# Linear attention feeding an expert layer: reciprocals spread over the features by DMA through DRAM, attention steps moved to the end of each block, transposes one a slot, row copies on ScalarE

## The chip, the cores and the metric

The kernel runs on one core of one Trainium2 chip. The metric is the device time of one execution in microseconds (us), lower is better. Each number is a median of several executions, compared with executions of the kernel before on the same chip. A ratio is the mean time of one kernel's fast runs over the mean of the other's fast runs of the same rounds, so it is not quite the ratio of the medians quoted beside it. A change counts as faster or slower only beyond 2%; below that the verdict is "same".

## The reference, cut to what matters

```
# attention: q, k, v are (batch 8, heads 8, seq 576, dim 64)
q_p = [relu(q) * cos, relu(q) * sin]       # 128 features; k_p likewise
kv  = sum over s of k_p x v ;  z = sum over s of k_p
x   = (q_p @ kv) / (q_p @ z + 1e-6)        # one denominator per batch, head and position
# x as 4608 tokens x 512 features (8 heads x 64), then 8 experts, F = 1024:
P   = sinkhorn(exp(x @ w_gate))            # 8 iterations
out = sum over e of P[:, e] * (relu(x @ w1[e]) @ w2[e])
```

The change is about the division. A denominator belongs to a head and a position, while the product to be divided has 64 features of that head. Its reciprocal therefore has to be repeated over 64 partitions before VectorE can multiply.

## The kernel before

The first part of the kernel runs in seven blocks. Block j does the first expert's two products for 512 tokens: slots 0 to 7 are eight groups of four matmuls (w1) with a ReLU on ScalarE into `hT`; slots 8 to 15 are eight groups of four matmuls (w2) whose results go to `acc`. Between the slots the pieces of the attention of batch b = j + 1 are put in: `prep_*` (cos and sin products on VectorE), `turn` (transposes of q, three matmuls each), `sums` (kv and z), `denominators`, and four `attend`s, one for each pair of heads. Work on TensorE, VectorE and ScalarE is bound to the written order. The loads that GpSimd issues are not.

```python
def denominators(b):
    ...                                    # 24 matmuls into den_ps
    ve.tensor_scalar(out=den, in0=den_ps, scalar1=1e-6 / XS, ...)
    ve.reciprocal(out=den, in_=den)        # 96 x 192: row 32*j + r is head r % 8, third j
    ve.tensor_copy(out=hi, in_=den)        # fp16 high part
    ve.scalar_tensor_tensor(out=hl, ...)   # high part or remainder, by row
    hls[b] = hl

def attend(b, hk):
    parts = ((0, 2 * C3), (2 * C3, C))     # 384 and 192 positions
    rb_ps = [ps_s.tile(...) for _ in parts]          # ps_s: four PSUM banks
    rb = rb_pool.tile([P, C * HP], FP32)
    for i, (c0, c1) in enumerate(parts):
        for j in range(c0 // C3, c1 // C3):
            te.matmul(out=rb_ps[i][...], lhsT=spread[0:96, j, hk], rhs=hls[b])   # spread by matmul
        se.copy(out=rb[:, c0 * HP : c1 * HP], in_=rb_ps[i][...])
    num_ps = [ps_s.tile(...) for _ in parts]
    for i, (c0, c1) in enumerate(parts):
        ...                                          # two matmuls: kv x q, one for each head
        ve.tensor_tensor(out=xT[...], in0=num_ps[i][...], in1=rb[...], op=ALU.mult)

# schedule of block j, b = j + 1 (cut)
at(j, 0, prep_q, b, 3); at(j, 1, prep_kv, b, 3)
at(j, 1, sums, b, 0);   at(j, 3, sums, b, 1)
for i, (hk, k_) in enumerate(turns[2:]):
    at(j, i // 2, turn, b, hk, k_)                   # two transposes a slot
at(j, 5, denominators, b)
for hk in range(HK):
    at(j, FT + 2 * hk, attend, b, hk)                # slots 8, 10, 12, 14
...                                                  # loads at slots 0, 2; prep of b + 1 at slots 6 to 15
# end of a w2 group: even rows by ScalarE, odd rows by VectorE
se.copy(out=acc(g), in_=y_ps) if g % 2 == 0 else ve.tensor_copy(out=acc(g), in_=y_ps)
```

The softmax here doesn't subtract the row's maximum and nothing guards it: scores larger than these inputs give would overflow.

Of the kernel before, what the change touches and what calls it, by code (L numbers as in the profile page):

```python
# [10 lines left out]
FP32 = mybir.dt.float32  # L11
F16 = mybir.dt.float16
# [13 lines left out]
def kernel(  # L26
# [10 lines left out]
    nc = tc.nc  # L37
    P = nc.NUM_PARTITIONS

    B, H, S, D = q.shape  # L40
    E, Dm, F = moe_w1.shape
    N = B * S
    HP = P // 2
    assert Dm == H * D and 2 * D == P and H % 2 == 0 and S % HP == 0
    HK = H // 2
    C = S // HP
# [3 lines left out]
    FT = F // P  # L50
    TCH = 512
# [12 lines left out]
    dram = ctx.enter_context(tc.tile_pool(name="dram", bufs=2, space=bass.MemoryType.DRAM))  # L64
# [6 lines left out]
    G_LO = NG - 4  # L71
    acc_lo = acc_pool.tile([P, G_LO, Dm], FP32, name="acc_lo")
    acc_hi = acc_pool.tile([P, NG - G_LO, Dm], FP32, name="acc_hi")

    def acc(g):
        return acc_lo[:, g, :] if g < G_LO else acc_hi[:, g - G_LO, :]
# [69 lines left out]
    def ffn2(hT, w, c0, g, y_ps, fts):  # L146

        for ft in fts:
            te.matmul(
                out=y_ps,  # L150
                lhsT=hT[:, ft, c0 : c0 + P],
                rhs=w[1][:, ft, :],
                start=(ft == 0),
                stop=(ft == FT - 1),
            )
        if FT - 1 in fts:

            if g % 2 == 0:
                se.copy(out=acc(g), in_=y_ps)
            else:  # L160
                ve.tensor_copy(out=acc(g), in_=y_ps)
# [10 lines left out]
    with ExitStack() as p1:  # L172
        hA = p1.enter_context(tc.tile_pool(name="hA", bufs=1))
        cs_pool = p1.enter_context(tc.tile_pool(name="cs_pool", bufs=1))
# [2 lines left out]
        qp_pool = p1.enter_context(tc.tile_pool(name="qp_pool", bufs=3))  # L177
        qT_pool = p1.enter_context(tc.tile_pool(name="qT_pool", bufs=6))
        kv_pool = p1.enter_context(tc.tile_pool(name="kv_pool", bufs=2))
        rb_pool = p1.enter_context(tc.tile_pool(name="rb_pool", bufs=2))  # L180
        ps_y = p1.enter_context(tc.tile_pool(name="ps_y", bufs=2, space=bass.MemoryType.PSUM))
        ps_s = p1.enter_context(tc.tile_pool(name="ps_s", bufs=4, space=bass.MemoryType.PSUM))

# [4 lines left out]
        def load(b, half, names="qkv"):  # L188
# [25 lines left out]
            out=ident[:], in_=ones_sq[:], pattern=[[-1, P]], compare_op=ALU.is_equal,  # L214
# [13 lines left out]
        def keep_busy(n):  # L228
# [12 lines left out]
            out=wrap[:], in0=gidx[:], scalar1=float(S), scalar2=None, op0=ALU.is_ge  # L241
# [3 lines left out]
            out=sval[:], in0=wrap[:], scalar=-float(S), in1=gidx[:],  # L245
# [13 lines left out]
        C3 = C // 3  # L259
# [7 lines left out]
        with nc.allow_low_precision("sums of zeros and ones"):  # L267
            ve.tensor_reduce(
                out=lo[:], in_=rows[:, :, 1, :], axis=AX.XY, op=ALU.add, negate=True
# [3 lines left out]
                out=sel[:], in0=rows[:, 0:3, 0, :], in1=rows[:, 0:3, 1, :], op=ALU.add  # L273
            )
        ve.tensor_copy(
            out=spread.rearrange("p j hk hh d -> p (j hk hh) d"),
            in_=sel[:].rearrange("p j h -> p (j h)").unsqueeze(2).to_broadcast([P, 3 * H, D]),
# [9 lines left out]
        ve.tensor_copy(out=wg[:], in_=wg_ld[:])  # L287


        kps, qps, qTs, kvs, hls = {}, {}, {}, {}, {}  # L290
        v_augs = [cs_pool.tile([P, C, D + 2], F16, name=f"v_aug{i}") for i in range(4)]
        for t in v_augs:
            ve.memset(t[:, :, D : D + 1], 1.0 / XS)

# [82 lines left out]
        def denominators(b):  # L377

            zsel = kvs[b][1]
            den_ps = ps_s.tile([P, 512], FP32, name="small_ps")  # L380
            for h in range(H):
                hk, hh = h // 2, h % 2
                for j in range(3):
                    te.matmul(
                        out=den_ps[32 * j : 32 * j + 32, 0 : C3 * HP],
                        lhsT=zsel[:, h, :],
                        rhs=qTs[b, hk][:, j * C3 : (j + 1) * C3, hh * HP : (hh + 1) * HP],
                        start=(h == 0),
                        stop=(h == H - 1),
                    )  # L390
            den = kv_pool.tile([96, C3 * HP], FP32, name="den")
            ve.tensor_scalar(
                out=den[:], in0=den_ps[0:96, 0 : C3 * HP], scalar1=1e-6 / XS, scalar2=None,
                op0=ALU.add,
            )
            ve.reciprocal(out=den[:], in_=den[:])

            hi = kv_pool.tile([96, C3 * HP], F16, name="hi")
            ve.tensor_copy(out=hi[:], in_=den[:])
            hl = kv_pool.tile([96, C3 * HP], F16, name="hl")  # L400
            ve.scalar_tensor_tensor(
                out=hl[:], in0=hi[:], scalar=lo[0:96], in1=den[:], op0=ALU.mult, op1=ALU.add
            )
            hls[b] = hl

        def attend(b, hk):

            parts = ((0, 2 * C3), (2 * C3, C))
            rb_ps = [ps_s.tile([P, 512], FP32, name="small_ps") for _ in parts]
            rb = rb_pool.tile([P, C * HP], FP32, name="rb")  # L410
            for i, (c0, c1) in enumerate(parts):
                for j in range(c0 // C3, c1 // C3):
                    te.matmul(
                        out=rb_ps[i][:, (j * C3 - c0) * HP : ((j + 1) * C3 - c0) * HP],
                        lhsT=spread[0:96, j, hk].rearrange("p hh d -> p (hh d)"),
                        rhs=hls[b][:],
                        start=True,
                        stop=True,
                    )
                se.copy(out=rb[:, c0 * HP : c1 * HP], in_=rb_ps[i][:, 0 : (c1 - c0) * HP])  # L420
            num_ps = [ps_s.tile([P, 512], FP32, name="small_ps") for _ in parts]
            for i, (c0, c1) in enumerate(parts):
                for hh in range(2):
                    te.matmul(
                        out=num_ps[i][hh * HP : (hh + 1) * HP, 0 : (c1 - c0) * HP],
                        lhsT=kvs[b][0][:, hk, hh, :],
                        rhs=qTs[b, hk][:, c0:c1, hh * HP : (hh + 1) * HP],
                        start=True,
                        stop=True,
                    )  # L430
                ve.tensor_tensor(
                    out=xT[:, hk, b * S + c0 * HP : b * S + c1 * HP],
                    in0=num_ps[i][:, 0 : (c1 - c0) * HP],
                    in1=rb[:, c0 * HP : c1 * HP],
                    op=ALU.mult,
                )
# [22 lines left out]
        NS = 2 * FT  # L459
        todo = {}  # L460

        def at(block, slot, fn, *args):
            todo.setdefault((block, slot), []).append((fn, args))

        turns = [(hk, i) for hk in range(HK) for i in range(3)]
# [17 lines left out]
        for hk in range(HK):  # L483
# [5 lines left out]
            if hk < 2:  # L489
                prep_q(0, hk + 2)  # L490
        denominators(0)
        keep_busy(36)

# [6 lines left out]
        for hk in range(HK):  # L500
# [7 lines left out]
            for kt in ((), (0,), (1,), (2, 3))[hk]:  # L508
                for ft, h_ps in enumerate(first_ps):
                    te.matmul(  # L510
                        out=h_ps[:],
# [10 lines left out]
        ahead = (  # L522
            (prep_k, 0), (prep_q, 0), (prep_k, 1), (prep_kv, 0), (prep_q, 1), (prep_k, 2),
            (prep_kv, 1), (prep_q, 2), (prep_k, 3), (prep_kv, 2),
        )
        for j in range(B):
            b = j + 1
            if j == 0:

                at(0, 4, lambda: begun.append(sums_begun(1, 0)))  # L530
                at(0, 5, lambda: sums_made(1, 0, begun[2]))
                at(0, 6, lambda: begun.append(sums_begun(1, 1)))
                at(0, 7, prep_q, 1, 0)
                at(0, 7, prep_q, 1, 1)
                for hk in range(HK):
                    for i in range(3):
                        at(0, 7 + hk, turn, 1, hk, i)
                    if hk == 0:
                        at(0, 7, lambda: sums_made(1, 1, begun[3]))
                    if hk < 2:  # L540
                        at(0, 7 + hk, prep_q, 1, hk + 2)
                at(0, 10, denominators, 1)
                at(0, 11, gates, 0)
                for hk in range(HK):
                    at(0, min(13 + hk, 15), attend, 1, hk)
            elif b < B:
                at(j, 0, prep_q, b, 3)
                at(j, 1, prep_kv, b, 3)
                at(j, 1, sums, b, 0)
                at(j, 3, sums, b, 1)  # L550
                for i, (hk, k_) in enumerate(turns[2:]):
                    at(j, i // 2, turn, b, hk, k_)
                at(j, 5, denominators, b)
                for hk in range(HK):
                    at(j, FT + 2 * hk, attend, b, hk)
            if j:
                at(j, 6, gates, j)
            if b + 1 < B:
                for half in range(2):
                    at(j, 2 * half if j else 3, load, b + 1, half)  # L560
                for i, (fn, hk) in enumerate(ahead):
                    at(j, NS - 10 + i if j else 11 + i // 2, fn, b + 1, hk)
                for hk, k_ in turns[:2]:
                    at(j, NS - 1, turn, b + 1, hk, k_)
        y_pss = {}
        for j in range(B - 1):
            if j:
# [494 lines left out]
    while stream:  # L1062
        _, pair, name = stream.pop(0)
# [32 lines left out]
```

## Time and profile before

| what | before |
|---|---|
| time | 1003.37 us (1002.86 to 1003.73, 4 runs) |
| span of the profiled run, granted TensorE clock (1 is full speed) | 1000.8 us, 0.997 |
| blocks 0 to 6 | 23.66, 22.25, 22.19, 22.29, 22.20, 22.29, 21.85 us |
| from the first `H` of the next part to the end | 815.5 us |

A block is measured in the timeline, from ScalarE's first ReLU into `hT` to that of the next block. The seven blocks lie between 28.5 and 185.3 us. The change touches only blocks 1 to 6 and what is prepared for them.

The page of the kernel before, its first table: busy time and share of the span of each engine.

```profile
PE 981.3 (98%) x8062; PEld 689.3 (69%) x8062; DVE 829.2 (83%) x1862; ACT 574.7 (57%) x1284; POOL 60.3 (6%) x82
```

The chain of waits of the kernel before (start, length, what). TensorE's (PE) groups carry the chain. At the end of each block it passes through VectorE (DVE) for a while; the block's period can be read from the repeats of the same piece.

```profile
72.22 0.98 PE y_ps L100 x4
...
73.84 0.75 DVE k_p L100
...
93.80 0.61 PE small_ps L100 x7
94.42 0.98 PE y_ps L100 x4
95.42 0.37 DVE acc_lo L100
96.03 0.75 DVE k_p L100
...
118.33 0.75 DVE k_p L100
```

The period is 22.2 to 22.3 us. In the timeline of TensorE, one attend looks as follows: three spreading matmuls with `hl`, the four with `kv_sb`, then the next w2 groups.

```profile
113.48 0.41 PE L100 MATMUL small_ps<-hl,acc_hi 96*128 96x192 f16 x3
113.83 0.44 PE L100 MATMUL small_ps<-q_pT,kv_sb 128*64 128x384 f16 x4
114.19 1.90 PE L100 MATMUL y_ps<-w2e,hT 128*128 128x512 f16 x8
```

The three spreading matmuls put off what follows by 113.83 - 113.48 = 0.35 us. They are what the change takes away from TensorE, four times a block. The SP queue has no DMA to issue in this part.

### The profile page before, as it was taken

To read this page: it belongs to the slowest core of one execution; us is meant where nothing else is said; L and a number is where in the kernel's file an instruction comes from. 1 tells how busy PE (TensorE), PEld (TensorE's weight loads), DVE (VectorE), ACT (ScalarE), POOL (GpSimd) and SP (SyncE) were. 2 spreads that over 40 slices of the span, in tenths; PEclk is the share of its full clock that TensorE was granted. 3 is DMA by queue.
4 is the path that set the end of the run, shared out by engine and by line. 5 is a ranking of instruction groups with operands and counts; after the bars stand their busy time and mean duration, and the time that the engine had idled before them with its cause. 6 is when DMAs were issued, how large, how long until landed. Compare 5 with 4: busy or idle time off the path is not lost.

```text
span 1000.8 us, 20629 instructions
## 1 busy us (share of the span) xinstructions
PE 981.3 (98%) x8062; PEld 689.3 (69%) x8062; DVE 829.2 (83%) x1862; ACT 574.7 (57%) x1284; POOL 60.3 (6%) x82
## 2 busy tenths in 40 slices
PE   7999999989999999999999999999999999999997
PEld 6455555446777777777777777777777777777775
DVE  5888777588989888888879878988789888988886
ACT  5766666447777555555555555555555555555551
POOL 6412200001000000000000000000000000000001
PEclk9999999999999999999999999999999999999999
DMA  9966610534002331034013320043113400104535
GB/s 165 206 92 87 87 23 1 105 70 82 33 25 51 65 66 48 26 76 80 25 48 67 60 55 26 25 90 66 41 33 67 90 25 25 48 25 111 130 89 124
DMA packets 51922, 66.50 MB, mean 66 GB/s; under 512 B 4848, under 2 KB 43760, under 8 KB 51824
## 3 DMA queue, kind: packets, MB, share of 16 engines
q0 software_dynamic: 27232, 30.94, 20.0%
q1 hardware_dynamic: 24352, 33.98, 12.4%
q8 instruction: 63, 1.03, 0.4%
q10 hardware_dynamic: 240, 0.26, 0.1%
q14 instruction: 35, 0.29, 0.1%
HBM read 83.12 MB, written 12.98 MB: 96 GB/s over the span
## 4 chain that ended last, share of the span: by engine, by line
PE 72%; issue 21%; DVE 4%; ACT 1%; DMA 1%; POOL 1%; POOLq 0%; ACTq 0%; DVEq 0%
PE rows_ps L100 25%; PE h_ps L100 21%; PE copied_ps L100 8%; PE p_ps L100 8%; PE y_ps L100 5%; PE small_ps L100 5%; DVE k_p L100 1%; DMA v_ld<-in_v_dram 1%; DVE q_pT L100 1%; DVE q_p L100 0%; DVE den L100 0%; DVE xT L100 0%; DVE acc_lo L100 0%; DVE P_tok L100 0%; DVE v_aug_240 L100 0%
## 5 line engine op out<-in xcount | busy, mean ns | idle before, releaser
L762 DVE SCALAR_TENSOR_TENSOR acc_lo<-rows_ps,P_tok,acc_lo 128x512 f32<-128x512 f32 (+1 forms) x322 | 203.1, 639 | 74.8 <-PE rows_ps L100 74.7
L100 PEld LDWEIGHTS <-H 128*128 128x128 f16 x2080 | 203.0, 98 | 83.1 <-issue 1.2
L100 PEld LDWEIGHTS <-w1e 128*128 128x128 f16 x1632 | 155.9, 98 | 59.2 <-issue 4.9
L100 PE MATMUL h_ps<-xT,w1e 128*128 128x384 f16 (+1 forms) x616 | 152.9, 350 | 0.0
L730 ACT ACTIVATE H<-h_ps 128x384 f16<-128x384 f32 x144 | 70.6, 490 | 95.1 <-PE h_ps L100 95.1
L100 PE MATMUL rows_ps<-w2e,H 128*128 128x256 f16 (+1 forms) x568 | 91.2, 285 | 0.0
L711 ACT COPY copied_ps<-h_ps 128x384 f32<-128x384 f32 x144 | 67.5, 469 | 35.3 <-PE h_ps L100 35.3
L721 ACT ACTIVATE H<-copied_ps 128x384 f16<-128x384 f32 x144 | 70.8, 492 | 20.4 <-PE copied_ps L100 20.4
L100 PE MATMUL copied_ps<-xT,w1e 128*128 128x384 f16 x336 | 82.1, 326 | 0.0
L100 PE MATMUL copied_ps<-w2e,H 128*128 128x256 f16 x504 | 75.6, 272 | 0.0
L762 DVE SCALAR_TENSOR_TENSOR acc_lo<-copied_ps,P_tok,acc_lo 128x256 f32<-128x256 f32 x126 | 60.0, 476 | 0.6 <-PE copied_ps L100 0.2
L762 DVE SCALAR_TENSOR_TENSOR acc_hi<-rows_ps,P_tok,acc_hi 128x512 f32<-128x512 f32 (+1 forms) x56 | 41.3, 737 | 20.4 <-PE rows_ps L100 19.6
L777 DVE TENSOR_TENSOR H<-H 128x512 f16<-128x512 f16 x125 | 52.6, 421 | 2.6
L100 PE MATMUL y_ps<-w2e,hT 128*128 128x512 f16 x224 | 54.7, 380 | 0.0
L804 ACT COPY copied_ps<-rows_ps 128x256 f32<-128x256 f32 x111 | 39.7, 357 | 17.6 <-PE rows_ps L100 17.6
L100 ACT ACTIVATE hT<-h_ps 128x512 f16<-128x512 f32 x54 | 32.3, 600 | 17.0 <-PE h_ps L100 16.6
L100 DVE TENSOR_TENSOR xT<-small_ps,rb 128x384 f16<-128x384 f32 x64 | 26.2, 451 | 16.6 <-ACT rb L100 16.5
L118 POOL DMA_DIRECT2D w1e<-in_moe_w_dram x11 | 8.3, 763 | 509.0 <-DVE T_3_5030 L670 92.4
L100 PEld LDWEIGHTS <-hT 128*128 128x128 f16 x224 | 19.5, 98 | 25.0 <-issue 5.8
L100 ACT COPY rb<-small_ps 128x384 f32<-128x384 f32 x64 | 22.4, 402 | 22.7 <-PE small_ps L100 22.6
L100 DVE TENSOR_SCALAR q_pT<-small_ps 128x384 f16<-128x384 f32 x46 | 25.0, 552 | 9.3 <-PE small_ps L100 8.7
L100 ACT ACTIVATE H<-h_ps 128x384 f16<-128x384 f32 (+1 forms) x40 | 21.3, 532 | 15.4 <-PE h_ps L100 14.7
(2459 smaller groups left out, 2065.8 us busy)
## 6 DMA issues: line engine op xcount, KB each, us to landing
out_dram<-acc_lo SPq DMA_DIRECT2D x62, 128.0 KB, 2.4
w1e<-in_moe_w_dram POOLq DMA_DIRECT2D x7, 1024.0 KB, 8.9
w2e<-in_moe_w_dram POOLq DMA_DIRECT2D x7, 1024.0 KB, 9.5
k_ld<-in_k_dram POOLq DMA_DIRECT2D x16, 288.0 KB, 6.4
v_ld<-in_v_dram POOLq DMA_DIRECT2D x16, 288.0 KB, 7.3
q_ld<-in_q_dram POOLq DMA_DIRECT2D x16, 288.0 KB, 6.8
w1e<-in_moe_w_dram POOLq DMA_DIRECT2D x4, 256.0 KB, 10.4
w2e<-in_moe_w_dram POOLq DMA_DIRECT2D x4, 256.0 KB, 10.9
```

The source lines that it names most:

```text
L100: i = getattr(self.engine, name)(*args, **kwargs)
L118: nc.gpsimd.dma_start(out=w[0][:, :, f0:f1], in_=view[:, :, f0:f1])
L711: se.copy(out=Y[:, 0:TU], in_=X[:, 0:TU])
L721: se.activation(out=h11, in_=Y[:, 0:TU], func=AF.Relu)
L730: se.activation(out=h12, in_=X[:, 0:TU], func=AF.Relu)
L762: ve.scalar_tensor_tensor(out=a, in0=rows, scalar=P_tok[:, g, self.e : self.e + 1], in1=a, op0=ALU.mult, op1=ALU.add,)
L777: i = (nc.gpsimd if self.last else ve).tensor_tensor(out=out_, in0=in0, in1=in1, op=op)
L804: se.copy(out=self.W, in_=self.U)
```

## The change

The intent is to free TensorE and ScalarE from spreading the reciprocals. For batches 2 to 7 the 96 x 192 reciprocals are stored in DRAM, and eight DMA reads with a zero stride, one for each head, bring a head's row to its 64 partitions. A row lies in DRAM as three pieces of 192 numbers, 768 bytes each. A transfer's landing is the moment when all of it has arrived. To give the DMA time, the attends move to slots 12 to 15 and the denominators to slot 4; the preparation of the next batch begins at slot 4 and its transposes spread out, one a slot. ScalarE takes all the row copies of blocks 1 to 6.

```diff
-            if g % 2 == 0:
+            if g % 2 == 0 or TCH // P <= g < (B - 1) * TCH // P:
                 se.copy(out=acc(g), in_=y_ps)
@@ denominators, after the reciprocal
+            if b >= 2:
+                r = dram.tile([96, C3 * HP], FP32, name="r")
+                nc.sync.dma_start(out=r[:], in_=den[:])
+                for hk in range(HK):
+                    rb = rb_pool.tile([P, C * HP], FP32, name="rb")
+                    for hh in range(2):
+                        h = 2 * hk + hh
+                        nc.sync.dma_start(
+                            out=rb[hh * HP : (hh + 1) * HP, :].rearrange("p (j s) -> p j s", j=3),
+                            in_=r[:].rearrange("(j r) s -> r j s", r=32)[h : h + 1]
+                                .to_broadcast([HP, 3, C3 * HP]))
+                    rbs[b, hk] = rb
+                return
@@ attend: where rbs has the batch, no spreading matmul and no copy to rb
@@ schedule (cut; block 1 keeps its old start, since batch 2 was prepared the old way)
-                    at(j, i // 2, turn, b, hk, k_)
-                at(j, 5, denominators, b)
-                    at(j, FT + 2 * hk, attend, b, hk)
+                    at(j, 0, sums, b, 1)
+                    for i, (hk, k_) in enumerate(turns[8:]):
+                        at(j, i, turn, b, hk, k_, k_ != 1)
+                at(j, 5 if j == 1 else 4, denominators, b)
+                    at(j, 12 + hk, attend, b, hk)
+                            at(j, 11 + 2 * half, load, b + 2, half)
+                        (4, prep_k, 0), (5, prep_q, 0), (6, prep_kv, 0), ... (15, prep_q, 3)
+                        at(j, 8 + i, turn, b + 1, hk, k_, k_ != 1)
+                    at(j, 10, sums, b + 1, 0)
```

Other lines give `rb` four buffers and lend a part of `acc` to `v_aug` to make room; `v_aug` therefore shows as `acc_lo` in the profiles after.

More of the change, by code (lines that the diff above doesn't have):

```diff
@@ L179 @@
         kv_pool = p1.enter_context(tc.tile_pool(name="kv_pool", bufs=2))
-        rb_pool = p1.enter_context(tc.tile_pool(name="rb_pool", bufs=2))
+        rb_pool = p1.enter_context(tc.tile_pool(name="rb_pool", bufs=4))
         ps_y = p1.enter_context(tc.tile_pool(name="ps_y", bufs=2, space=bass.MemoryType.PSUM))
@@ L287 @@
         ve.tensor_copy(out=wg[:], in_=wg_ld[:])
-        kps, qps, qTs, kvs, hls = {}, {}, {}, {}, {}
-        v_augs = [cs_pool.tile([P, C, D + 2], F16, name=f"v_aug{i}") for i in range(4)]
+        kps, qps, qTs, kvs, hls, rbs = {}, {}, {}, {}, {}, {}
+        lent = acc_lo[:, G_LO - 4 : G_LO, :].rearrange("p g d -> p (g d)").bitcast(F16)
+        VA = C * (D + 2)
+        v_augs = [
+            lent[:, i * VA : (i + 1) * VA].rearrange("p (c d) -> p c d", d=D + 2)
+            for i in range(4)
+        ]
         for t in v_augs:
@@ L396, in denominators @@
             ve.reciprocal(out=den[:], in_=den[:])
+            if b >= 2:
[6 more added lines that the diff above has]
+                        nc.sync.dma_start(
+                            out=rb[hh * HP : (hh + 1) * HP, :].rearrange(
+                                "p (j s) -> p j s", j=3
+                            ),
+                            in_=r[:].rearrange("(j r) s -> r j s", r=32)[h : h + 1].to_broadcast(
+                                [HP, 3, C3 * HP]
+                            ),
+                        )
+                    rbs[b, hk] = rb
+                return
             hi = kv_pool.tile([96, C3 * HP], F16, name="hi")
@@ L408, in attend @@
             parts = ((0, 2 * C3), (2 * C3, C))
-            rb_ps = [ps_s.tile([P, 512], FP32, name="small_ps") for _ in parts]
-            rb = rb_pool.tile([P, C * HP], FP32, name="rb")
+            rb = rbs.pop((b, hk), None)
+            rb_ps = [ps_s.tile([P, 512], FP32, name="small_ps") for _ in parts if rb is None]
+            by_dma = rb is not None
+            if not by_dma:
+                rb = rb_pool.tile([P, C * HP], FP32, name="rb")
             for i, (c0, c1) in enumerate(parts):
+                if by_dma:
+                    break
                 for j in range(c0 // C3, c1 // C3):
@@ L546 @@
             elif b < B:
-                at(j, 0, prep_q, b, 3)
-                at(j, 1, prep_kv, b, 3)
-                at(j, 1, sums, b, 0)
-                at(j, 3, sums, b, 1)
-                for i, (hk, k_) in enumerate(turns[2:]):
-                    at(j, i // 2, turn, b, hk, k_)
-                at(j, 5, denominators, b)
+                if j == 1:
+                    at(j, 0, prep_q, b, 3)
+                    at(j, 1, prep_kv, b, 3)
+                    at(j, 1, sums, b, 0)
+                    at(j, 3, sums, b, 1)
+                    for i, (hk, k_) in enumerate(turns[2:]):
+                        at(j, i // 2, turn, b, hk, k_, k_ != 1)
+                else:
+                    at(j, 0, sums, b, 1)
+                    for i, (hk, k_) in enumerate(turns[8:]):
+                        at(j, i, turn, b, hk, k_, k_ != 1)
+                at(j, 5 if j == 1 else 4, denominators, b)
                 for hk in range(HK):
-                    at(j, FT + 2 * hk, attend, b, hk)
+                    at(j, 12 + hk, attend, b, hk)
             if j:
@@ L558 @@
             if b + 1 < B:
-                for half in range(2):
-                    at(j, 2 * half if j else 3, load, b + 1, half)
-                for i, (fn, hk) in enumerate(ahead):
-                    at(j, NS - 10 + i if j else 11 + i // 2, fn, b + 1, hk)
-                for hk, k_ in turns[:2]:
-                    at(j, NS - 1, turn, b + 1, hk, k_)
+                if j == 0:
+                    for half in range(2):
+                        at(0, 3, load, b + 1, half)
+                        at(0, 14 + half, load, b + 2, half)
+                    for i, (fn, hk) in enumerate(ahead):
+                        at(0, 11 + i // 2, fn, b + 1, hk)
+                    for hk, k_ in turns[:2]:
+                        at(0, NS - 1, turn, b + 1, hk, k_)
+                else:
+                    if b + 2 < B:
+                        for half in range(2):
+                            at(j, 11 + 2 * half, load, b + 2, half)
+                    for slot, fn, hk in (
+                        (4, prep_k, 0), (5, prep_q, 0), (6, prep_kv, 0), (6, prep_k, 1),
+                        (7, prep_q, 1), (8, prep_kv, 1), (9, prep_k, 2), (10, prep_q, 2),
+                        (11, prep_kv, 2), (11, prep_k, 3), (13, prep_kv, 3), (15, prep_q, 3),
+                    ):
+                        at(j, slot, fn, b + 1, hk)
+                    for i, (hk, k_) in enumerate(turns[:8]):
+                        at(j, 8 + i, turn, b + 1, hk, k_, k_ != 1)
+                    at(j, 10, sums, b + 1, 0)
         y_pss = {}
```

## The prediction

> **What bounds the kernel now.** TensorE is 98% busy. The change touches the first part, blocks 1 to 6 (50 to 184 us), where each block interleaves 64 matmuls 128x512 of the first expert with the attention of the next batch. The chain of waits repeats every 22.2 us (`k_p` pieces at 73.84, 96.03, 118.33, 140.52): 17.4 us TensorE, and 4.8 us at the block's start through VectorE (k_p, v_aug, q_pT, q_p, ...). TensorE works meanwhile: from the starts of its groups in the timeline (95.2 to 107.7) it loses only about 0.9 us a block. Busy per block (25-us windows, scaled): VectorE 17 us, ScalarE 14 us.
>
> **Removed (6 batches).**
> - TensorE: 12 spreading matmuls a batch. In the timeline each group of three delays the next by 0.35 us (113.48 to 113.83): 1.0 to 1.4 us a batch, on the critical path, 6 to 8 us in all.
> - ScalarE: copies to rb, 4 x (0.478 + 0.325) = 3.2 us a batch.
> - VectorE: hi and hl 0.67 us, two row copies 1.37 us (to ScalarE at 0.585 each), two turns 1.1 us (to ScalarE at 0.5): 3.1 us a block. ScalarE nets about -1 us. Both off the path but for the start-up stall.
> - The stall: preparation begins at slot 4 instead of 6 and mostly ends inside the previous block: 4 to 5 us in all (block 1 keeps part).
>
> Sum: 10 to 13 us.
>
> **Added.** Per batch a 72 KB store, then 8 broadcast reads, 1.18 MB in 768-byte pieces on the SP queue, 96 per DMA engine. Hardware-queue packets take 46 ns (1024 B) and 65 ns (1536 B), so I estimate 40 ns: 4 us of all engines a block; the loads take about 11 us (96 packets of 1152 B at 107 to 118 ns). Issue is 0.32 us each (x_saved), landing 1.8 to 2.4 us. Counted from slot 4's start, the reciprocals end at 3.5 us, the first rb should land at 9 us and the last at 11 to 16; they are needed at 10.7 to 15. The margin is thin: later batches' loads issue whenever a buffer comes free (they wait on q_p in the waits), near slot 8, amid the reads. The Trainium skill (DMA: Bandwidth & Descriptors, "Issuing engines are not separate DMA queues") says both queues run on the same 16 engines and interleave; load-heavy slices here show a DMA share of 0.9. I charge 0 to 1 us a block. Attends in the last four slots also crowd VectorE (4 x 0.9 us), and the next block's first product needs the last xT part at once: 0.2 to 0.4 us a block.
>
> **Prediction.** 1003.2 - 12.5 + 3 = about 993.5 us; 989.5 to 998.5 holds it 8 times in 10. Everything after block 6 only shifts. Faster by over 2%: 0.03; within 2%: 0.93; slower: 0.04.
>
> **What would show it.** Period 20.2 to 21 us in blocks 2 to 5; no VectorE pieces at block starts in the chain; rb copies and hl gone; xT multiplications waiting for nothing, or, if DMA is late, for DMA rb. Block 1 stays near 22 us, block 6 is shortest. From expert 2 on, both traces are the same but for a shift.
>
> **What would make it wrong.** rb landing after its attend (broadcast reads slower than 40 ns a piece, or starved by loads): each late microsecond costs up to 6 us, and 2 us undoes the gain. VectorE overfull in slots 12 to 15, so that the stall moves to the block's end. Larger TensorE stalls than I count would make the gain larger.

## The result, and the profile after

The changed kernel takes 1015.36 us (1012.33 to 1016.75, 4 runs) against 1003.37: ratio 1.0116, 95% interval 1.0092 to 1.0139. By the 2% rule that is "same", but it is slower, clear of the noise, where about 1% faster was forecast.

| | before | after | difference |
|---|---|---|---|
| up to the first block | 28.52 | 29.91 | +1.39 |
| block 0 | 23.66 | 23.72 | +0.06 |
| block 1 | 22.25 | 29.65 | +7.40 |
| block 2 | 22.19 | 26.38 | +4.19 |
| block 3 | 22.29 | 26.15 | +3.86 |
| block 4 | 22.20 | 20.99 | -1.21 |
| block 5 | 22.29 | 20.65 | -1.64 |
| block 6 | 21.85 | 21.07 | -0.78 |
| rest | 815.5 | 815.3 | -0.3 |

The differences add up to the 13.0 us between the two profiled spans (1013.8 and 1000.8). Blocks 4 and 5 are what was hoped for; blocks 1 to 3 lose 15.5 us together. What sets 4 and 5 apart is that the last load of q, k and v has been issued (at 135.25 us, the end of block 3), so that none runs beside their reads.

The chain of waits after the change, block 2. It leaves TensorE at the reciprocal (`den`), and passes through the store `r`, SP's issues and one read of `rb` before VectorE's `xT` lets TensorE go on.

```profile
89.30 1.36 DVE den L100
...
90.68 1.60 DMA r<-den
...
92.29 0.57 SPq L411
92.86 0.05 issue
92.92 0.60 SPq L411
93.52 0.05 issue
93.57 0.60 SPq L411
94.17 0.04 issue
94.22 10.12 DMA rb<-r
...
104.45 0.57 DVE xT L100
105.02 0.04 issue
105.07 0.55 PE small_ps L100 x5
105.61 1.23 PE y_ps L100 x4
```

One read takes 10.12 us from its issue to its landing. At the same time GpSimd issues loads; its timeline, in the same stretch:

```profile
93.25 0.71 POOL L192 DMA_DIRECT2D q_ld<-in_q_dram  x1 [8.87 <-DVE q_p L100]
93.96 0.72 POOL L192 DMA_DIRECT2D k_ld<-in_k_dram  x1
94.67 0.72 POOL L192 DMA_DIRECT2D v_ld<-in_v_dram  x1
```

The bracket says what the issue had waited for: VectorE's `q_p`, that is, the buffer to come free. The slots 11 and 13 that the program writes for the loads mean nothing to GpSimd, which is not bound to the written order.

The DMA queues after, from 68 to 76 us (block 1, loads running): packets, MB, share of the 16 engines. q0 is GpSimd's queue, q1 SP's.

```profile
q0 software_dynamic: 753, 0.82, 71.2%
q1 hardware_dynamic: 705, 0.51, 27.4%
```

The same from 147 to 153 us (block 4, no loads):

```profile
q1 hardware_dynamic: 1507, 1.07, 75.6%
```

SP's reads move 0.51 MB in 8 us beside the loads, 0.064 MB a us, and 1.07 MB in 6 us alone, 0.18 MB a us: over this window they run at about a third of their speed. The figure depends on the window. From 72 to 76 us it is 0.35 MB in 4 us, nearer half:

```profile
q0 software_dynamic: 478, 0.52, 78.7%
q1 hardware_dynamic: 494, 0.35, 36.7%
```

These two lines also show how the engines are shared: both queues move about as many packets. So it is in block 2 (98 to 102 us: 488 of the loads, 449 of the reads) and in block 3 (124 to 128 us: 520 and 491). In these stretches a piece of a read gets through for about every piece of a load, and the pieces of the loads are the larger ones (1152 bytes).

The windows after (stretch, then busy time with counts of PE, PEld, DVE, ACT and POOL, granted clock, DMA share, GB/s; the share adds up the packets' times, which can overlap, so it can pass 1):

```profile
72.00:76.00 4.00, 0.01 (x2) 0.01 (x1) 0.62 (x2) 0.23 (x1) 0.00 (x0) 0.91 1.15 218
76.00:82.00 6.00, 6.00 (x25) 2.19 (x25) 3.37 (x9) 1.56 (x3) 1.43 (x2) 0.50 0.61 126
```

TensorE stands still for the whole of 72 to 76, and when it works again its clock is 0.50. In the chain, four w2 matmuls take 1.71 us instead of 0.86 there. So a late `rb` is paid twice, in waiting and in half clock.

The waits after, from 50 to 200 us (who waited for whom: us in total, times, longest), and the page's table of DMA issues (KB each, median us to landing):

```profile
DVE xT L100 <- DMA rb<-r: 28.9, 11, 8.7
```

Of these, 19.2 us (8 times, 5.8 at the longest) lie in blocks 1 to 3. The wait of 8.7 us is in block 6, which has nothing to prepare meanwhile.

```profile
rb<-r SPq DMA_DIRECT2D x48, 144.0 KB, 5.5
```

### The profile page after: what moved, and what is told of

It reads as the page before. It is cut to its first block, busy times and chain, and to the rows that moved or that the text cites. A ratio compares the mean times of both kernels' runs of the same rounds, so it can differ in the third digit from the quotient of the medians.

```text
span 1013.8 us, 20476 instructions
## 1 busy us (share of the span) xinstructions
PE 983.8 (97%) x7990; PEld 687.2 (68%) x7990; DVE 811.9 (80%) x1826; ACT 571.2 (56%) x1260; POOL 60.3 (6%) x82
## 4 chain that ended last, share of the span: by engine, by line
issue 75%; PE 15%; DMA 4%; DVE 3%; POOL 2%; SPq 1%; ACT 1%; POOLq 0%; DVEq 0%; ACTq 0%
PE h_ps L100 5%; PE small_ps L100 4%; DMA rb<-r 3%; PE y_ps L100 3%; PE rows_ps L100 1%; DVE den L100 1%; SPq L411 1%; DMA r<-den 1%; DMA k_ld<-in_k_dram 1%; POOL w2e L124 0%; DVE xT L100 0%; PE copied_ps L100 0%; POOL w1e L118 0%; POOL acc_lo L975 0%; DVE P_tok L100 0%
## 5 line engine op out<-in xcount | busy, mean ns | idle before, releaser
L100 PE MATMUL y_ps<-w2e,hT 128*128 128x512 f16 x224 | 59.8, 395 | 0.0
L811 DVE SCALAR_TENSOR_TENSOR acc_hi<-rows_ps,P_tok,acc_hi 128x512 f32<-128x512 f32 (+1 forms) x56 | 41.3, 738 | 20.5 <-PE rows_ps L100 19.7
L100 ACT ACTIVATE q_pT<-small_ps 128x384 f16<-128x384 f32 x62 | 29.8, 493 | 27.0 <-PE small_ps L100 26.7
L100 ACT ACTIVATE hT<-h_ps 128x512 f16<-128x512 f32 x54 | 32.3, 600 | 19.7 <-PE h_ps L100 18.6
L100 PEld LDWEIGHTS <-q_p 128*128 128x128 f16 x288 | 21.3, 102 | 17.3 <-issue 6.7
L100 PEld LDWEIGHTS <-hT 128*128 128x128 f16 x224 | 20.2, 100 | 18.1 <-issue 2.5
L100 PE MATMUL small_ps<-ident,q_p 128*128 128x128 f16 x288 | 30.5, 229 | 1.7 <-ACT q_pT L100 1.0
```

What stands on the lines that cost most here:

```text
L100: i = getattr(self.engine, name)(*args, **kwargs)
L811: ve.scalar_tensor_tensor(out=a, in0=rows, scalar=P_tok[:, g, self.e : self.e + 1], in1=a, op0=ALU.mult, op1=ALU.add,)
```

## The experiments

Theory 1: `rb` lands after its attend, because the reads share the DMA engines with the loads and because the path from reciprocal to `rb` is longer than reckoned; TensorE then waits, and falls to half clock. Rival: the new schedule itself (attends crowded at the end, more work beside them) makes the waits. Twelve kernels ran, in three groups of four with three rounds each. The runs of the kernel before in the three groups gave medians of 1003.34, 1002.95 and 1003.17 us.

### e1_matmul: the new schedule without the DMA

```diff
-            if b >= 2:
+            if b >= B:        # every batch spread by matmul
```

> The changed kernel's schedule (attends last, early preparation, one turn a slot, ScalarE's copies), with the reciprocals of every batch still spread by matmul. Theory 1 (rb arrives late by DMA, and the half clock that follows a stall makes it worse): no DMA is waited for, so blocks 1 to 3 fall from 29.7, 26.4, 26.2 us to about 22; the twelve matmuls a batch come back (1.0 to 1.4 us a block on the 20.65 us of the undisturbed blocks), so about 998 to 1003 us in all. Rival (the new schedule itself crowds VectorE and PSUM at the block's end): stays at 1010 us or above, with the stalls at the block ends.

Measured: 1008.68 us, ratio 1.0052 (1.0038 to 1.0067). Blocks 1 to 6: 25.65, 23.18, 23.28, 23.18, 23.28, 19.81. This lies between the two forecasts. The 26 to 30 us blocks are gone and no half clock falls in the blocks, so those came with the DMA. But the schedule by itself is no gain either: against the kernel before it costs about 1 us a block in blocks 2 to 5 and 3.4 in block 1, and gains 2.0 in block 6. The chain of waits of this run shows where, at the attends:

```profile
93.88 0.49 ACT rb L100
94.37 0.04 issue
94.42 0.33 PE small_ps L100 x3
```

TensorE waits for ScalarE's copy of `rb` out of PSUM, the memory that TensorE writes its products to.

### e2_noload: no loads beside the reads

```diff
             for name in names:
+                if b >= 3:    # batches 1 and 2 again: a wrong result on purpose
+                    for i in range(2):
+                        loaded[name, b, 2 * half + i] = kept[name, 2 - b % 2, 2 * half + i]
+                    continue
```

> The changed kernel, but q, k and v of batches 3 to 7 are not loaded: the tiles of batches 1 and 2 are used again (a wrong result on purpose). Theory 1 with the loads as the cause of the lateness: blocks 1 to 5 all come to 20.7 to 22 us, xT never waits for DMA rb by more than 1 us, about 992 to 997 us. If the path from the reciprocals to rb is too long by itself (store, eight issues, landing), blocks 1 to 3 stay above 24 us and the total stays above 1005. Rival (schedule): no change against the changed kernel, 1012 to 1017.

Measured: 996.79 us (996.47 to 997.85), ratio 0.994 (0.9924 to 0.9957), result wrong as intended. Blocks 1 to 6: 23.16, 20.56, 20.65, 20.56, 20.66, 20.58. This decides for theory 1: taking away the loads, and nothing else, takes 18.6 us from the changed kernel, and 18.7 us in the six blocks of the profiles. The group of `rb` in this run says how long an undisturbed read takes:

```profile
DMA to landing us min/median/max: 4.1/4.4/5.6
```

With the loads these were 4.0, 5.5 and 11.0 us. In blocks 1 to 5 `xT` never waits for DMA `rb`, as forecast. All of that wait, 9.4 us with a longest of 7.8, lies in block 6 (160 to 182 us), which has nothing to prepare and so waits for the path itself: it takes 20.58 us here and 18.46 in e9_rows_den2 below, where the path starts earlier.

### e3_oldsched: the DMA without the new schedule

```diff
 # the kernel before; for batches 2 to 7 denominators() stores r and reads rb as in the change,
 # and attend() uses it; denominators at slot 5, attends at slots 8, 10, 12, 14 as before
```

> The kernel before with its own schedule (attends at slots 8, 10, 12, 14, denominators at slot 5, copies shared with VectorE), only the reciprocals of batches 2 to 7 go through DRAM by DMA. Theory 1: the first attend comes 3 slots after the reciprocals, while store, issue and landing took 9 us and more, so every block waits 6 us or more: 1035 to 1070 us, with half clock after the stalls. Rival (the schedule is at fault, the DMA is harmless): faster than before by 5 us or so.

Measured: 1024.83 us, ratio 1.0218 (1.0203 to 1.0234), slower. Blocks 1 to 6: 25.13, 25.88, 25.33, 25.48, 25.26, 27.94. The direction is theory 1's; the size is smaller than forecast (about 3 us a block, and 6 only in block 6). The reads landed after 4.2 us in the median and 5.0 at most, as they do with no loads beside them, so the loss here comes from the path and not from the loads. The late attends are needed if the DMA is to be used at all.

### e4_rows: larger pieces, fewer reads

```diff
-                r = dram.tile([96, C3 * HP], FP32, name="r")
-                nc.sync.dma_start(out=r[:], in_=den[:])
+                r = dram.tile([H, 3, C3 * HP], FP32, name="r")       # a row of 576 for each head
+                for j in range(3):
+                    nc.sync.dma_start(out=r[:, j, :], in_=den[32 * j : 32 * j + H, :])
+                rb = rb_pool.tile([P, HK, C * HP], FP32, name="rb")
+                heads = r[:].rearrange("(hk hh) j s -> hh hk (j s)", hh=2)
+                for k0 in (0, 2):
+                    for hh in range(2):                                # four reads, not eight
+                        nc.sync.dma_start(
+                            out=rb[hh * HP : (hh + 1) * HP, k0 : k0 + 2, :],
+                            in_=heads[hh : hh + 1, k0 : k0 + 2].to_broadcast([HP, 2, C * HP]))
```

> The changed kernel, but the DRAM tile holds one row of 576 numbers a head (three small stores of 8 partitions), and four reads of 2304-byte pieces bring all of rb in place of eight reads of 768-byte pieces: a third of the pieces, half the issues. Theory 1 with the turn-taking of pieces between the two kinds of queue and the serial issue (0.65 us each, 5.2 us a batch) as the mechanism: rb lands 4 to 8 us earlier, blocks 1 to 3 fall below 24 us, total 993 to 1002 us. If bytes rather than pieces and issues count: blocks 1 to 3 stay above 25 us and the total above 1008.

Measured: 1004.82 us (1000.92 to 1005.77), ratio 1.0009 (0.9988 to 1.0031). Blocks 1 to 6: 25.25, 23.11, 22.49, 20.56, 20.66, 21.12. The same bytes reach `rb` with a third of the pieces and half the issues, and about 11 of the 12 us lost come back. Blocks 2 and 3 came out as expected, block 1 did not (25.25, not under 24), and the total is 3 us above the range. Number of pieces and number of issues were changed together, so their shares stay open. The trace says something of the pieces: beside the loads of block 2 (92 to 96 us) the reads moved 0.46 MB in 4 us with 218 packets, for 386 of the loads, where the changed kernel's moved 0.32 MB with 449 (98 to 102 us). The larger pieces carry some 40% more there, not three times as much.

### e5_gate: loads held until rb has landed

```diff
+                if b - 2 in landed:        # in load(): wait for the last rb of batch b - 2
+                    tc.add_manual_dep(i.ins, landed[b - 2].ins.name, Sync, ...)
```

> The changed kernel, all data loaded, but the loads of batch b+2 are issued only when the last rb of batch b has landed, so the two kinds of transfer no longer share the engines. Theory 1 (contention with the loads is what made rb late): blocks 2 and 3 fall from 26 us to 20.6 to 21.5 as in the run without loads, block 1 to about 23; total 996 to 1000 us. If the loads now come late for the next batch's preparation, blocks 2 to 4 show waits of k_ld and stay at 22 to 24 us. If the changed kernel's loss had another cause (the missing loads helped only because VectorE or GpSimd had less to do), no change: 1010 or above.

Measured: 1004.53 us (1003.02 to 1006.06), ratio 1.0016 (1.0 to 1.0032). Blocks 1 to 6: 22.87, 22.43, 22.57, 23.65, 22.08, 20.42. With all data loaded and the result correct, moving the loads in time alone takes away the 26 to 30 us blocks. The total misses its range by 4.5 us, and blocks 2 and 3 theirs by 1 us: the rest of the gain of e2_noload does not come. The forecast's other way to fail, waits of `k_ld`, is not it (0.6 us in all). The held loads run on into the next block, and there the store `r` takes its place among them: in blocks 2 to 5 it landed after 4.3 to 4.9 us, against 1.6 in the changed kernel. `xT` still waits 25.1 us in all for `rb`.

### e6_rows_gate: both repairs

The edit is e4_rows and e5_gate together.

> Both repairs: whole rows of 2304 bytes in four reads, and the loads held until the last rb has landed. Reads are all issued 2.5 us after the store lands, so the loads start about slot 12 instead of slot 15 and come in time. Blocks 2 to 6 at 20.6 us, block 1 about 23; 995 to 999 us, faster than both kernels but by less than 1%.

Measured: 999.25 us (998.11 to 1001.46), ratio 0.9966 (0.9948 to 0.9984). Blocks 1 to 6: 22.70, 21.65, 20.80, 21.26, 21.67, 19.10. The total lies just above the range, and blocks 2, 4 and 5 are 0.7 to 1.1 us longer than the forecast's 20.6. The chain of waits shows what is left: the last of the three small stores took 1.25 us in e4_rows (block 2),

```profile
87.69 1.25 DMA r<-den
```

and takes 2.58 here, beside the held loads.

```profile
84.23 2.58 DMA r<-den
```

### e7_early_matmul: no DMA, attends where they were, the rest of the change kept

```diff
-            if b >= 2:
+            if b >= B:
-                    at(j, 12 + hk, attend, b, hk)
+                    at(j, FT + 2 * hk, attend, b, hk)
```

> No DMA: reciprocals spread by matmul for every batch, attends at slots 8, 10, 12, 14 as in the kernel before, but preparation early, one turn a slot and ScalarE's copies as in the changed kernel. If the loss of the run with matmuls and late attends (23.2 us a block) came from attends in adjacent slots, which share four PSUM banks and wait for ScalarE's rb copies, the blocks fall to 21.3 to 22.2 us (22.25 before, minus up to 0.9 us of start-up stall): 997 to 1003 us. If it came from early preparation or from ScalarE's copies, they stay at 23 us and the total at 1008.

Measured: 1006.68 us (1006.35 to 1007.03), ratio 1.0037 (1.002 to 1.0054). Blocks 2 to 5 at 22.96 to 23.07. Adjacent attends were not the reason for e1_matmul's loss; spreading them out brought 0.2 us a block.

### e8_copies: the changed kernel, row copies shared again

```diff
-            if g % 2 == 0 or TCH // P <= g < (B - 1) * TCH // P:
+            if g % 2 == 0:
```

> The changed kernel with only the row copies put back (even rows ScalarE, odd rows VectorE). Theory 1: this part matters little, since late rb sets the pace: within 4 us of the changed kernel, blocks 4 and 5 at 20.6 to 21 us still. A VectorE-bound end of block (the rival) would make blocks 4 and 5 longer by about 1 us.

Measured: 1015.85 us, ratio 1.0127 (1.0105 to 1.0149); the changed kernel had 1.0116. Blocks 4 and 5: 20.67 and 20.78. As forecast, the row copies made no difference that these runs can show.

### e9_rows_den2: larger pieces, and the denominators two slots earlier

```diff
 # on top of e4_rows
-                        at(j, i, turn, b, hk, k_, k_ != 1)
-                at(j, 5 if j == 1 else 4, denominators, b)
+                        at(j, i // 2, turn, b, hk, k_, k_ != 1)
+                at(j, 5 if j == 1 else 2, denominators, b)
```

> The whole-row kernel (2304-byte pieces, four reads, loads not held) with the denominators of batches 3 to 7 at slot 2 in place of 4, the last four turns two a slot. Theory 1: store and reads start 2 slots (2 us) earlier, rb comes 2 us earlier against its attends, and more of the reads are done before the loads of the slot-7 buffers start; blocks 2 and 3 fall from 23.1 and 22.5 to about 20.7 us: 1000 to 1002 us against 1004.8. If it stays at 1004, the time from the reciprocals is not what counts.

Measured: 996.89 us (996.78 to 998.52), ratio 0.9945 (0.9928 to 0.9962). Blocks 1 to 6: 24.60, 20.69, 21.04, 20.70, 20.70, 18.46. That is 3 us better than forecast; blocks 2 and 3 are where they were expected, and the rest is block 6, which had waited for the path alone. The result is correct, loads and reads may overlap as they come, and with e10_rows_gate_den2 it is the fastest correct version, 0.55% below the kernel before. The waits for `rb`, 54 to 200 us:

```profile
DVE xT L100 <- DMA rb<-r: 3.2, 1, 3.2
```

### e10_rows_gate_den2: the same, with the loads held

> Whole rows, loads held until the last rb has landed, and denominators at slot 2. The remaining waits of the held version (xT for DMA rb, 10.9 us in all, blocks 2 to 5 at 20.8 to 21.7 us) go away: blocks 2 to 5 at 20.6 us as in the run without loads, total 995 to 998 us, the fastest so far.

Measured: 997.62 us (996.61 to 998.26), ratio 0.9946 (0.9932 to 0.9961). Blocks 1 to 6: 22.69, 21.75, 20.82, 21.82, 20.95, 18.46. The waits were expected to go and did not: `xT` still waits 10.5 us for `rb`. Holding the loads helps block 1, which keeps its denominators at slot 5, and hurts blocks 2 and 4.

### e11_early_shared: no DMA, only the earlier preparation

```diff
 # on top of e7_early_matmul: row copies as before, transposes alternate between the engines as before
-            if g % 2 == 0 or TCH // P <= g < (B - 1) * TCH // P:
+            if g % 2 == 0:
-                        at(j, 8 + i, turn, b + 1, hk, k_, k_ != 1)
+                        at(j, 8 + i, turn, b + 1, hk, k_)
```

> No DMA; matmul spreading, attends at slots 8, 10, 12, 14, early preparation and one turn a slot, but row copies and turns shared between ScalarE and VectorE as in the kernel before. If ScalarE's extra load (two more copies of 0.585 us and two more turns of 0.5 us a block, in line ahead of the rb copies) made the version with ScalarE's copies 23 us a block, this falls to 21.3 to 22.2 us a block and 996 to 1003 us. If early preparation itself costs (VectorE's work now beside the attends), it stays at 22.5 to 23 us a block and 1005 us or so.

Measured: 1007.51 us (1006.68 to 1008.21), ratio 1.0046 (1.0031 to 1.0061). Blocks 2 to 5 at 22.99 to 23.11. So ScalarE's share was not it. The waits from 80 to 150 us hold a line that the kernel before does not have in the same stretch:

```profile
PE small_ps L100 <- ACT rb L100: 2.3, 12, 0.3
```

TensorE waits at nearly every attend for ScalarE's `rb` copy to give a bank of PSUM back. The 2.3 us fall in some three blocks, 0.7 to 0.8 us each, which is about what a block is longer by (0.8 us). By the code, an attend with matmul spreading takes four of the four `ps_s` banks, and a transpose, which now falls between the attends, a fifth. That is a reading of the code and this line; no run with more banks was made, because all eight are taken.

### e12_den2: the changed kernel, denominators two slots earlier

The edit is the one of e9_rows_den2, on the changed kernel itself.

> The changed kernel as it is (768-byte pieces, eight reads, loads not held), only the denominators of batches 3 to 7 at slot 2. Block 1 stays at 29 us; blocks 2 and 3 lose 2 us of lateness each and some half clock, from 26.2 to about 24: 1009 to 1013 us. If lateness had nothing to do with the start of the reads, no change: 1015.

Measured: 1007.21 us (1005.58 to 1008.46), ratio 1.0042 (1.0027 to 1.0057). Blocks 1 to 6: 29.39, 24.42, 22.77, 20.79, 20.69, 18.98. Block 1, whose denominators did not move, is as slow as ever; block 2 gains 2 us as forecast and block 3 more, 3.4 us. The total comes out 2 us better than the range; block 6, which the forecast left out, gains 2.1.

## Why the prediction was wrong

- **What bounds the kernel: right.** TensorE carries the chain, and the part after block 6 only shifts: 815.5 us before, 815.3 after.
- **The gain when nothing is late: right in place, too large.** The prediction had 10 to 13 us. In e2_noload blocks 1 to 6 take 126.2 us against 133.1 before: 6.9 us. Blocks 2 to 5 gain 1.6 us each, as forecast (a period of 20.2 to 21 us). Block 1 takes 0.9 us more, not less: it finishes batch 2's transposes and starts batch 3's.
- **Where that gain comes from: only half right.** The prediction added up the spreading matmuls and the start-up stall as if each could be had alone. e1_matmul, e7_early_matmul and e11_early_shared show that earlier preparation with matmul spreading costs 0.7 to 1 us a block in blocks 2 to 5, and e3_oldsched that the DMA with the old schedule costs about 3 us a block. Only the two together win.
- **The step that failed: "I charge 0 to 1 us a block" for reads and loads on the same engines.** Against the run without loads, the same kernel with loads is 6.5, 5.8 and 5.5 us longer in blocks 1, 2 and 3. The length of the path alone was not the error. Counted from slot 4's start, as in the prediction, the first `rb` was to land at 9 us and the last at 11 to 16, and they were needed at 10.7 to 15. In block 4, with no loads, they landed at 9.9 and 15.0 us. In block 2, beside the loads, they landed at 12.3 and 20.5.
- **Two terms of that path were too small, and its wide range hid it.** The issue was put at 0.32 us a read from the plain stores; the broadcast reads took 0.57 us at least and 0.61 in the median, so that in block 4 eight of them kept SP busy for 5.16 us. The landing was put at 1.8 to 2.4 us; it was 4.4 in the median with no loads beside it (e2_noload), and up to 11.0 with them. That the quiet landings still fell where they were forecast is partly luck.
- **The mechanism was named and then priced too low.** The prediction said that loads would issue as soon as a buffer comes free, near slot 8, amid the reads, and cited the Trainium skill (DMA: Bandwidth & Descriptors, "Issuing engines are not separate DMA queues"): both kinds run on the same 16 engines and interleave. The trace agrees: 27.4% of the engines' time for SP's reads beside the loads, 75.6% alone. What was missing is the step from "they interleave" to a rate: about one read piece for every load piece, which left the reads a third to a half of their speed for as long as loads were queued.
- **A cost that was not in the sum: half clock after a stall.** The Trainium skill (TensorE: Matmul & The Clock Gate, "Part 1: The HAM clock gate") says that TensorE falls to half rate after an idle window of about 3.4 us. In block 1 the trace agrees: idle from 72 to 76 us, clock 0.50 from 76 to 82, four matmuls at 1.71 us for 0.86. In blocks 2 and 3 shorter pauses, 3.25 and 2.95 us, were followed by half clock too. The prediction reckoned "each late microsecond costs up to 6 us" over six blocks, one for one; block 1, with a pause of 4.1 us, came out 6.5 us longer than without loads. No run measured the half clock on its own, but the record bounds it. In blocks 1 to 3 the clock was 0.50 for 17.1 us (75.25 to 82.08, 105.97 to 109.39, 129.87 to 136.69), which by this estimate cost at most half of that, 8.5 us; TensorE's waits for `xT` there were 10.9 us. The three blocks are 17.8 us longer than in e2_noload, whose blocks have no half clock.
- **Three blocks, not six.** The prediction charged every block. Blocks 4 and 5, after the last load, ran at 20.99 and 20.65 us.
- **Small parts: right.** The row copies were called off the path, and moving them to ScalarE changes nothing measurable (e8_copies). VectorE's crowding in slots 12 to 15, named as a risk, did not show in blocks 4 and 5.
- **Open.** The +1.39 us ahead of block 0 lies in a stretch whose order of work the change leaves alone. The clock record of that profile has a longer stretch of half clock there than the one of before (6.8 and 3.4 us), but runs of the kernel before differ among themselves too (1001.70 us at clock 1.000, 1004.15 at 0.996). All twelve profiles of the new schedule have the longer stretch, and the two of the old one (before and e3_oldsched) the shorter, so it may belong to the schedule; why it would is not settled. Also open are the shares of pieces and of issues in e4_rows, and the bank shortage read from e11_early_shared.

## What to carry to other kernels

Before work is moved from a busy engine to a DMA, look at what the DMA queues carry at that very moment, and take the landing time from transfers under that load, not from quiet ones; on a queue that is not bound to the program's order, the time at which a buffer comes free is the time of issue. If such a transfer is late, cut it into fewer and larger pieces and start it earlier: here that turned a loss of 1.2% into a gain of 0.55%, with the same bytes reaching the tile. And test the parts of a change together as well as alone, because schedule and DMA each lost by itself.

## What the Trainium skill lacked or had wrong

- DMA: Bandwidth & Descriptors, "Issuing engines are not separate DMA queues", calls the sequencer's time to start a DMA "usually small relative to the DMA itself". Here it was not: eight reads of 144 KB took SP 5.16 us to issue in block 4, about as long as the 16 engines on average were busy with them (54.7% of the 9 us from 146 to 155, 4.9 us). The store of 72 KB took 0.31 us to issue.
- The same page has a rule for how an engine takes turns between queues, but no measured rate for a stream of small pieces beside a stream of larger ones on another queue. Here 768-byte reads fell from 0.18 MB a us to between 0.064 and 0.09 beside loads of 1152-byte pieces, and four reads of 2304-byte pieces in place of eight brought back some 11 us of the kernel.
- No page has a landing time for several broadcast reads issued one behind the other: 4.1 to 5.6 us for 144 KB each with no loads running (e2_noload).
- TensorE: Matmul & The Clock Gate, "Part 1: The HAM clock gate", does not say how much work within a window keeps the full clock. Here half clock followed pauses of 3.25 and 2.95 us, and in e3_oldsched one of 1.39 and one of 0.67 us close together (95 to 98.5 us), but no half clock followed one of 1.94 us in e5_gate.
